# A decode step of attention with a bilinear GLU on one core: the first weight load is placed elsewhere in the ring, its projections are seven even runs, the last V heads are grouped 1-2-1, and the last gather is four steps

## The chip, the cores and the metric

The kernel runs on one core of one Trainium2 chip. The metric is the device time in microseconds (us) of one execution; a kernel's time is the median of several executions without the profiler. One further execution was profiled. The core has TensorE (PE), VectorE (DVE), ScalarE (ACT), GpSimd (POOL) and SyncE (SP); here SP issues nearly all DMA transfers, in the order in which they are written.

## The reference

One token for each of two sequences (B = 2, D = 512), all float32:

```python
xn = layernorm(x)
q = (xn @ wq)                       # 32 heads of 128
k = k_cache[:, :, 8192 - 2048:, :]  # the last 2048 positions
v = v_cache[:, :, 8192 - 2048:, :]
scores = einsum("bhqd,bhkd->bhqk", q, k) * 128 ** -0.5
o = einsum("bhqk,bhkd->bhqd", softmax(scores), v)
h = (xn @ w_gate) * (xn @ w_up)     # 1376 wide
out = x + o.reshape(B, 1, 4096) @ wo + h @ w_down
```

Every weight and every cached key and value is used once, so some 160 MB go from HBM to the core for two small output rows.

## The kernel before

**Staging.** The host lays all inputs but `x` out as one stream in the order of use. In SBUF one large tile, `step` (in the code `ring`), holds whatever is loaded: every load is one DMA of 128 rows with a run of columns for each partition. The ring has a place for four V heads (`C_V`, 16384 columns, 4096 for each head), one for four K heads (`C_K`, 16384) and 12288 columns for pairs of w_q and w_o chunks and the early rows of w_down. The table in `loads()` (L47) gives each load its semaphore, its first column and its fields. `x` is the first load (w_gate, w_up, the first chunk of w_q, and constants, 13082 columns), `k0` the four K heads of group 0, `v0` its V heads, `w1` early rows of w_down with w_q and w_o chunks, then `k1`, `v1`, `k2`, `v2`, and so on. The last ones are `v7` (V heads 28 and 29), `v30`, `v31`, and four small loads `d0`, `wo7`, `d1`, `d2`, which hold rows of w_down and the last chunk of w_o.

**Work.** Eight groups of four heads. For a group PE projects q (`q_ps`, matmuls against `xn`), multiplies q with K (`s_ps`, 32 matmuls of 512 columns), and after the softmax multiplies the weights `p` with V (`o_ps`, 32 matmuls). The profile counts two passes for each float32 matmul, so four matmuls appear as x8 and 32 as x64. `gather` takes the four blocks of `o_ps` that belong together (DVE `om`, then `red`), PE picks the rows (`pk`), DVE scales them (`oT`), and PE multiplies them with w_o (`acc`), which DVE adds to `xr`. Ahead of group 0 stand the projections for gate and up: three runs each of 459 columns. ACT copies a gate run from `q_ps` to `g`; DVE multiplies an up run with it into `h`. In group 0 PE also multiplies early rows of w_down (section `e`, `acc<-step,hT`), ahead of the V matmuls; after the last V head it multiplies further rows (section `r`) and at the end of the program the rest (section `tail`, `s_ps`).

**What sets the order.** `Program` records every operation with what it reads and writes; `plan` makes a wait of every dependence that is not known to be met. PE runs its sections in a loop whose waits (`hold`) compare a semaphore with a register. Since a wait in the loop is for one semaphore, a `relay` stands in for others: POOL waits for them and then writes a small memset into `none`, whose end raises the one that PE waits for (`wq`, `wo`, `V2`, `V3`). A load is issued by SP as soon as PE has read what lay at its place. SP works in order: a load that waits holds up all those behind it. `x` starts at `C_GU`, which is `C_V`, so that it fills the place of V, while `w1` goes to that of the pairs; `v0` is issued in the main loop after the projection of q for group 0.

Every instruction has the line of the helper that records it, L107, in the profile.

Of the kernel before, what the change touches and what calls it, by code (L numbers as in the profile page):

```python
# [5 lines left out]
ALU = mybir.AluOpType  # L6
# [19 lines left out]
CK = B * W  # L26
GW = -(-F // 3)
GU = [(w, n) for w in range(2) for n in range(3)]
CX = N + 4 + 4 + 2
# [17 lines left out]
def loads():  # L47


    v, k = [("v", h) for h in range(H)], [("k", h) for h in range(H)]  # L50
    pair = [(("wq", g), ("wo", g - 1)) for g in range(NG)]
    wd = {i: ("wd", i) for i in range(NFC + 1)}
    last = H - HG
    out = {
        "x": (None, C_GU, [("gu", t) for t in GU] + [("wq", 0), ("c", 0)]),
        "k0": ("K", C_K, k[:HG]),
        "w1": (None, C_E - len(EARLY) * D, [wd[i] for i in EARLY] + [*pair[2], *pair[1]]),
    }
    for g in range(NG - 1):
        if g:  # L60
            out[f"k{g}"] = ("K", C_K, k[g * HG : g * HG + HG])
        out[f"v{g}"] = ("V", C_V, v[g * HG : g * HG + HG])
        if g == 2:
            out["w2"] = (None, C_E, [*pair[4], *pair[3]])
        if g == 4:
            out["w4"] = (None, 0, [("wo", 6), ("wq", 7), *pair[6], *pair[5]])
# [31 lines left out]
class Op:  # L98
    def __init__(self, eng, method, args, kw, deps, dma, tag, place, holds, late):
        self.eng, self.method, self.args, self.kw, self.late = eng, method, args, kw, late  # L100
        self.deps, self.dma, self.tag, self.place, self.holds = deps, dma, tag, place, holds
# [21 lines left out]
class Program:  # L123


    def __init__(self, nc):
        self.nc = nc
        self.eng = {"PE": nc.tensor, "DVE": nc.vector, "ACT": nc.scalar,
                    "POOL": nc.gpsimd, "SP": nc.sync}
        self.ops, self.seen = [], {}  # L130
        self.tags = {}
        self.tag, self.also, self.held, self.late = None, [], [], None
        self.section, self.step = None, 0
# [23 lines left out]
    def put(self, eng, method, writes, reads, args, kw, dma=False):  # L157
# [20 lines left out]
        if tag is None:  # L178
            tag = f"d{i}" if dma else eng
        else:  # L180
            self.tags.setdefault(tag, []).append(i)
        place, holds = None, []
# [4 lines left out]
        late, self.late = self.late, None  # L187
        self.ops.append(Op(eng, method, args, kw, deps, dma, tag, place, holds, late))
        return i
# [9 lines left out]
    def plan(self, looped):  # L199
# [15 lines left out]
        for i, o in enumerate(ops):  # L215
# [20 lines left out]
            if o.dma and o.tag in self.tags:  # L236
                prev = [key_of(j) for j in self.tags[o.tag] if j < i]
                assert all(know.get(key, 0) >= val for key, val in prev), (o.tag, i)
# [7 lines left out]
        for i, o in enumerate(ops):  # L246
# [4 lines left out]
            else:  # L251
                continue
            value[o.tag] = at[i] = value.get(o.tag, 0) + step
        return waits, at

    def emit(self, looped, control):
# [10 lines left out]
        def give(i, first=None):  # L267
# [11 lines left out]
            if i in at:  # L279
                ins.then_inc(sem[o.tag], 16 if o.dma or o.tag in BY_16 else 1)  # L280

# [19 lines left out]
        once = {}  # L301
        for i in own["SP"][:3]:
            give(i)
# [7 lines left out]
        with nc.body("straight", valid_engines=list(kinds.values())):  # L311
            for e in kinds:
                here = self.eng[e].mark_branch_hint_location()
                for i in own[e][3 if e == "SP" else 0 :]:
                    if i not in stores:
                        give(i)
# [50 lines left out]
def steer(prog, regs, run):  # L367
# [8 lines left out]
    with nc.body("pe_q", valid_engines=only):  # L376
        here = pe.mark_branch_hint_location()
        regs["from"] = pe.snap(at, min_val=0, max_val=RING - 4 * FB)
        regs["by"] = pe.snap(step, min_val=GW, max_val=FB)
        run("q")  # L380
        pe.reg_add(n, n, 1)
        pe.br_lt(n, len(GU) + 2, on_true="pe_n", on_false="pe_k")
    with nc.body("pe_n", valid_engines=only):
        pe.reg_add(at, at, NC * GW)
        pe.br_lt(n, len(GU) + 1, on_true="pe_q", on_false="pe_c")
    with nc.body("pe_c", valid_engines=only):
        pe.reg_mov(step, FB)
        pe.br("pe_q")
    with nc.body("pe_k", valid_engines=only):
        pe.reg_mov(at, then)  # L390
# [24 lines left out]
def build(nc, stream, x_nat, out):  # L415
# [27 lines left out]
    hT = pr.sb("hT", [P, NFC + 1, 32])  # L443
    g_sb = pr.sb("g", [P, 3, GW])
    h_sb = pr.sb("h", [P, (NFC + 1) * P])
    o_out = red
# [25 lines left out]

    def relay(tag, *aps):
        nonlocal relays
        pr.also = list(aps)
        pool.memset(none[:, relays : relays + 1], 0.0, tag=tag)
        relays += 1
# [7 lines left out]
    issue("k0")  # L485
    issue("w1")
    for t, v in ((xr, 0.0), (eps_t, EPS), (xs, 0.0), (h_sb, 0.0), (zero, 0.0), (ones, 1.0),
                 (mt, 0.0), (qz, 0.0), (p_all, 0.0)):
        pool.memset(t, v)
    pr.load("ACT", xr[:B, :], x_nat)  # L490
    for t in (acc, q_ps, s_ps):
# [7 lines left out]
    dve.tensor_scalar(xs2, x2, total, None, ALU.subtract)  # L499
    dve.tensor_tensor(g_sb[:B, 0, 0:GW], xs2[:, 0:GW], xs2[:, 0:GW], op=ALU.mult)  # L500
    dve.tensor_tensor(
        g_sb[:B, 1, 0 : D - GW], xs2[:, GW:D], xs2[:, GW:D], op=ALU.mult
    )
    flat = g_sb.rearrange("p n i -> p (n i)")
    dve.tensor_reduce(var, flat[:B, 0:D], axis=AX.X, op=ALU.add)
    act.activation(std, var, AF.Sqrt, bias=eps_t[:B], scale=1.0 / D)
# [6 lines left out]
    def project(c0, step, *used):  # L513
        nonlocal n_run
        n_run += 1
        relay("wq", *used)
        pr.part("q")
# [8 lines left out]

    hh_ = h_sb[:B, 0 : 3 * GW].rearrange("p (n i) -> p n i", n=3)
    used = [xn]
    for i, (w, n) in enumerate(GU):
        project(C_GU + i * NC * GW, GW, got["gu", (w, n)], *used)  # L530
        wide = min(GW, F - n * GW)
        if w == 0:
            act.copy(g_sb[:B, n, 0:wide], q_ps[:B, 0:wide])
            used = [g_sb[:B, n, 0:wide]]
        else:
            dve.tensor_tensor(
                hh_[:, n, 0:wide], g_sb[:B, n, 0:wide], q_ps[:B, 0:wide], op=ALU.mult
            )
            used = [hh_[:, n, 0:wide]]
    pool.tensor_copy(cst, got["c", 0])  # L540
    pick, rmask, mask, id4 = (
# [3 lines left out]
    def queries(g):  # L545
        across(qt, q_ps.rearrange("p (h i) -> p h i", h=HG))
        at = qz[:, 0, 0:1]
# [61 lines left out]
    def gather(g):  # L609
        dve.tensor_tensor(  # L610
            om, o_ps.rearrange("p (r d) -> p r d", r=4),
            rmask.unsqueeze(2).to_broadcast([P, 4, DH]), op=ALU.mult,
        )
        dve.tensor_reduce(red, om.rearrange("p r d -> p d r"), axis=AX.X, op=ALU.add, tag="red")
        pr.part("g")
# [35 lines left out]
    for g in range(NG):  # L651
        c0 = C_Q0 if g == 0 else C_Q[(g - 1) % 2]
        project(c0, FB, ring[:, c0 : c0 + NC * FB], *used)
        queries(g)
        used = [qt]
# [20 lines left out]
        if g < NG - 1:  # L676
            for tag in ("V2", "V3"):
                relay(tag, got["v", g * HG])
            relay("wo", place)
# [4 lines left out]
        elif g == NG - 2:  # L684
            for name in ("v7", "v30", "v31"):
                issue(name)
# [22 lines left out]
def laid_out(x):  # L709
# [15 lines left out]
    wo = x["A_wo"].reshape(NG, HG, P, D)  # L725
    gu = [x[name].reshape(NC, P, F) for name in ("B_w_gate", "B_w_up")]
    wd = x["B_w_down"]

    def field(kind, i):
# [11 lines left out]
        if kind == "wd":  # L741
            return np.pad(wd[i * P : (i + 1) * P], ((0, max(0, (i + 1) * P - F)), (0, 0)))
        w, n = i
        part = gu[w][:, :, n * GW : min(n * GW + GW, F)]
        part = np.pad(part, ((0, 0), (0, 0), (0, GW - part.shape[2])))
        return part.transpose(1, 0, 2).reshape(P, NC * GW)

# [32 lines left out]
```

## Time and profile before

| what | value |
|---|---|
| median of 3 runs | 380.36 us (379.9 to 381.18) |
| the profiled execution | 382.39 us |
| its span on the core | 381.1 us |
| mean granted clock of PE | 0.821 |
| busy PE, DVE, ACT, POOL | 216.8, 61.1, 13.2, 15.7 us |
| read from HBM | 159.53 MB, 419 GB/s over the span |

Times in the profile count from the start of the span, which is 1.29 us shorter than the profiled execution. A row of the chain of waits has the start, the duration and what the chain went through; a row of the timeline adds the engine, the shapes and, in brackets, how long the engine was idle before it and what ended that. A row of the windows has a stretch of time, its length, the busy time of PE, PE's weight loads, DVE, ACT and POOL with their instruction counts (for one tile alone, of the engines that touch it), the granted clock of PE, the share of DMA and GB/s. A packet's bytes count where the packet starts, so that short windows jump between 0 and high values.

### The profile page before, as it was taken

Reading aid. Unit: us, or ns where it says so; the run is one execution under the profiler, and the core shown is the slowest. Engines: PE = TensorE matmul, PEld = TensorE weight load, DVE = VectorE, ACT = ScalarE, POOL = GpSimd, SP = SyncE. Lnnn points to the kernel's source line nnn. Section 1 sums busy time; section 2 is a strip of 40 time slices with the busy share of each in tenths; the row PEclk is TensorE's granted clock in tenths of the full one; section 3 lists DMA queues with packets and bytes.
Section 4 is the critical chain, followed back from the end, with each engine's and each line's share of the span. In section 5 each row is a group of like instructions: output and inputs, shape, how many; then the busy total and the mean of one; then the engine's idle time right before and its main releaser. Section 6 shows DMA issues by size and latency. Waiting matters only on the chain.

```text
span 381.1 us, 3091 instructions
## 1 busy us (share of the span) xinstructions
PE 216.8 (57%) x1296; PEld 52.0 (14%) x1296; DVE 61.1 (16%) x150; ACT 13.2 (3%) x26; POOL 15.7 (4%) x55
## 2 busy tenths in 40 slices
PE   0088877287718570850909771843373876186766
PEld 0011111021102120210202110200011212021211
DVE  0300142012201220120020212021020122012203
ACT  4001010000000000000000000000000000000000
POOL 3000000001000000020000000010000030000000
PEclk9999999578958996895776895668585889589998
DMA  9999959999999998999999999999999999998994
GB/s 352 462 427 398 433 207 433 440 440 440 440 440 440 440 440 385 495 440 440 427 420 392 413 440 440 433 447 440 440 440 440 441 440 433 440 440 371 411 422 187
DMA packets 3894, 159.62 MB, mean 419 GB/s; under 512 B 434, under 2 KB 562, under 8 KB 948
## 3 DMA queue, kind: packets, MB, share of 16 engines
q1 hardware_dynamic: 3888, 159.60, 97.4%
q8 instruction: 1, 0.02, 0.0%
q14 instruction: 1, 0.01, 0.0%
q10 hardware_dynamic: 4, 0.00, 0.0%
HBM read 159.53 MB, written 0.07 MB: 419 GB/s over the span
## 4 chain that ended last, share of the span: by engine, by line
DMA 71%; PE 26%; DVE 1%; issue 1%; ACT 0%; POOL 0%; POOLq 0%
DMA step<-in_stream_dram 71%; PE o_ps L107 18%; PE q_ps L107 7%; DVE h L107 0%; ACT g L107 0%; DVE red L107 0%; PE acc L107 0%; POOL none L107 0%; DVE om L107 0%; DVE xr L107 0%; PE s_ps L107 0%; PE pk L107 0%; DVE oT L107 0%; POOLq L275 0%
## 5 line engine op out<-in xcount | busy, mean ns | idle before, releaser
L107 PE MATMUL o_ps<-step,p 128*32 128x512 f32 x512 | 74.4, 743 | 55.3 <-DMA step<-in_stream_dram 55.3
L107 PE MATMUL s_ps<-step,qz 128*8 128x512 f32 x512 | 60.9, 631 | 39.6 <-DMA step<-in_stream_dram 33.2
L107 PE MATMUL q_ps<-step,xn 128*2 x112 | 56.7, 653 | 25.1 <-POOL none L107 25.1
L107 PEld LDWEIGHTS o_ps<-step,p 128*32 128x32 f32 x512 | 17.8, 133 | 106.2 <-DMA step<-in_stream_dram 59.2
L107 DVE TENSOR_TENSOR om<-o_ps,cst 128x512 f32<-128x512 f32 x8 | 5.5, 691 | 127.7 <-PE o_ps L107 127.7
L107 PEld LDWEIGHTS s_ps<-step,qz 128*8 128x8 f32 x512 | 14.1, 94 | 86.5 <-issue 76.3
L107 PEld LDWEIGHTS q_ps<-step,xn 128*2 128x2 f32 x112 | 9.8, 92 | 72.9 <-issue 72.9
L107 DVE TENSOR_REDUCE mt<-s_ps 128x1 f32<-128x512 f32 x8 | 5.5, 692 | 88.4 <-PE s_ps L107 88.4
L107 PE MATMUL acc<-step,oT 128*2 128x512 f32 x64 | 11.6, 809 | 5.6 <-POOL none L107 3.1
L107 POOL MEMSET none<- 128x1 f32 x36 | 2.6, 98 | 283.5 <-DMA step<-in_stream_dram 254.4
L107 DVE STREAM_TRANSPOSE qt<-q_ps 32x128 f32<-32x128 f32 x32 | 9.8, 307 | 26.5 <-PE q_ps L107 26.1
L107 PE MATMUL pk<-cst,red 128*128 128x8 f32 x16 | 3.2, 272 | 14.2 <-DVE red L107 14.2
L107 PE MATMUL tot<-rs,ones 128*128 128x8 f32 x16 | 3.9, 319 | 12.0 <-DVE rs L107 12.0
L107 POOL COPY step<-step 128x2048 f32<-128x2048 f32 x5 | 9.4, 1890 | 32.4 <-PE acc L107 32.4
L107 PE MATMUL top<-dg,ones 128*128 128x32 f32 x16 | 3.3, 287 | 10.3 <-DVE dg L107 10.3
L107 DVE TENSOR_TENSOR xr<-xr,acc 128x512 f32<-128x512 f32 x9 | 6.2, 688 | 17.7 <-PE acc L107 17.7
L107 ACT COPY qz<-qt 128x8 f32<-128x8 f32 x8 | 1.6, 204 | 213.2 <-DVE qt L107 213.2
L107 DVE TENSOR_REDUCE red<-om 128x128 f32<-128x512 f32 x8 | 8.2, 1019 | 0.3
L107 ACT ACTIVATE p<-t,zero 128x128 f32<-128x128 f32 x8 | 4.2, 522 | 105.2 <-DVE t L107 105.2
L107 DVE TENSOR_TENSOR h<-g,q_ps 2x459 f32<-2x459 f32 (+1 forms) x3 | 1.9, 621 | 33.5 <-PE q_ps L107 33.5
L107 DVE STREAM_TRANSPOSE sT<-s_ps 128x512 f32<-128x512 f32 x8 | 5.7, 708 | 0.0
L107 PEld LDWEIGHTS pk<-cst,red 128*128 128x128 f32 x16 | 2.5, 193 | 21.4 <-DVE red L107 21.4
(49 smaller groups left out, 44.6 us busy)
## 6 DMA issues: line engine op xcount, KB each, us to landing
step<-in_stream_dram SPq DMA_DIRECT2D x2, 4096.0 KB, 27.7
step<-in_stream_dram SPq DMA_DIRECT2D x1, 6541.0 KB, 18.6
step<-in_stream_dram SPq DMA_DIRECT2D x1, 6144.0 KB, 34.5
step<-in_stream_dram SPq DMA_DIRECT2D x1, 5376.0 KB, 49.8
step<-in_stream_dram SPq DMA_DIRECT2D x2, 2048.0 KB, 28.0
step<-in_stream_dram SPq DMA_DIRECT2D x1, 1024.0 KB, 22.3
step<-in_stream_dram SPq DMA_DIRECT2D x1, 768.0 KB, 20.2
step<-in_stream_dram SPq DMA_DIRECT2D x1, 512.0 KB, 23.1
```

Of the source, the lines that this page charges most:

```text
L107: return getattr(engine, self.method)(*args, **self.kw)
```

## The change

The places in the ring are arranged anew: V first, then 12288 columns for the pairs, then K. The first load `x` now starts at column 15551 and ends at 28645: only the first part of it, 833 columns of the first run, lies in the place of V, and the rest lies on the places of w_q, w_o and early w_down rows. gate, up and the first q chunk are put side by side (3264 columns) and cut into seven runs of 467 columns (`RUNS`, `GW`); all seven go through one ACT copy each into a tile `wide`, and the end of the copy raises `wq` itself, without a relay. DVE multiplies gate and up once, in `wide`. `v0` is issued after the first run, ahead of `w1`, and `w1` after the last run. The relays for `V2` and `V3` are replaced by two relays at the start, each of which counts for seven groups (`times`). The last V heads come as `v28`, `v29` (heads 29 and 30) and `v31`; accordingly PE waits for `V`, `V2`, `V3` ahead of heads 0, 1 and 3 of a group, where it was 0, 2 and 3. In the last group, `gather` is one multiplication by a column of the mask and three multiply-adds of 128 columns.

```diff
-GW = -(-F // 3)
-GU = [(w, n) for w in range(2) for n in range(3)]
+RUNS = 7
+WIDE = 2 * F + FB
+GW = -(-WIDE // RUNS)
...
-C_E = HG * D + NC * FB
-C_Q = (C_E + HG * D + NC * FB, C_E)
+PAIR = HG * D + NC * FB
+C_V, C_E = 0, HG * CK
+C_Q = (C_E + 2 * PAIR, C_E + PAIR)
 C_O = tuple(c + NC * FB for c in C_Q)
-C_V = C_O[0] + HG * D
-C_K = C_V + HG * CK
+C_K = C_E + 3 * PAIR
 RING = C_K + HG * CK
-C_GU = C_V
-C_Q0 = C_GU + len(GU) * NC * GW
-C_C = C_Q0 + NC * FB
+C_END = C_K - (FB - GW - CX)
+C_GU = C_END - CX - RUNS * NC * GW
...
-        "x": (None, C_GU, [("gu", t) for t in GU] + [("wq", 0), ("c", 0)]),
+        "x": (None, C_GU, [("gu", i) for i in range(RUNS)] + [("c", 0)]),
         "k0": ("K", C_K, k[:HG]),
-        "w1": (None, C_E - len(EARLY) * D, [wd[i] for i in EARLY] + [*pair[2], *pair[1]]),
+        "v0": ("V", C_V, v[:HG]),
+        "w1": (None, C_Q[1] - len(EARLY) * D, [wd[i] for i in EARLY] + [*pair[2], *pair[1]]),
...
-    out["v7"] = ("V", C_V, v[last : last + 2])
-    out["v30"] = ("V2", C_V + 2 * CK, v[last + 2 : last + 3])
+    out["v28"] = ("V", C_V, v[last : last + 1])
+    out["v29"] = ("V2", C_V + CK, v[last + 1 : last + 3])
     out["v31"] = ("V3", C_V + 3 * CK, v[last + 3 :])
...
     issue("x")
     issue("k0")
-    issue("w1")
...
+    for tag in ("V2", "V3"):
+        relay(tag, times=NG - 1)
...
-    used = [xn]
-    for i, (w, n) in enumerate(GU):
-        project(C_GU + i * NC * GW, GW, got["gu", (w, n)], *used)
-        wide = min(GW, F - n * GW)
-        if w == 0:
-            act.copy(g_sb[:B, n, 0:wide], q_ps[:B, 0:wide])
-            used = [g_sb[:B, n, 0:wide]]
-        else:
-            dve.tensor_tensor(
-                hh_[:, n, 0:wide], g_sb[:B, n, 0:wide], q_ps[:B, 0:wide], op=ALU.mult
-            )
-            used = [hh_[:, n, 0:wide]]
-    pool.tensor_copy(cst, got["c", 0])
+    for i in range(RUNS):
+        project(C_GU + i * NC * GW, GW, *([] if i else [got["gu", 0], xn]))
+        act.copy(
+            wide[:, i * GW : (i + 1) * GW], q_ps[0:32, 0:GW],
+            tag="wq" if i < RUNS - 1 else None,
+        )
+        if i == 0:
+            pool.tensor_copy(cst, got["c", 0])
+            issue("v0")
+    issue("w1")
...
-        if hh != 1:
-            pr.hold({0: "V", 2: "V2", 3: "V3"}[hh], g + 1, "landed")
+        if hh != 2:
+            pr.hold({0: "V", 1: "V2", 3: "V3"}[hh], g + 1, "landed")
...
+        else:
+            for r in range(4):
+                part, m = o_ps[:, r * DH : (r + 1) * DH], rmask[:, r : r + 1]
+                if r == 0:
+                    dve.tensor_scalar(om[:, 0, :], part, m, None, ALU.mult)
+                else:
+                    dve.scalar_tensor_tensor(
+                        red if r == 3 else om[:, r, :], part, m, om[:, r - 1, :],
+                        ALU.mult, ALU.add, tag="red" if r == 3 else None,
+                    )
...
         if g == 0:
-            issue("v0")
-            across(hT, h_sb.rearrange("p (c i) -> p c i", i=P))
+            dve.tensor_tensor(wide[:B, 0:F], wide[:B, 0:F], wide[:B, F : 2 * F], op=ALU.mult)
+            across(hT, wide[:, 0 : (NFC + 1) * P].rearrange("p (c i) -> p c i", i=P))
```

How it moves instructions is seen at three places. The first is the start of SP's queue, here before the change; a row has the operation, its tile, the partitions and columns, and the semaphores that it waits for (`s_PE` counts PE's matmuls). The loads are x, k0, w1, and then, in the row with x5, v0, k1, v1, k2, v2.

```order
L107 DMA step<-in_stream_dram 128x13082 [waits barrier_Pool_Activation_PE_DVE_SP_release]
L107 DMA step<-in_stream_dram 128x16384
L107 DMA step<-in_stream_dram 128x10752
L307 UNCONDITIONAL_BRANCH
L313 BRANCH_PREFETCH_HINT
L107 DMA step<-in_stream_dram 128x16384 [waits s_PE] x5
```

The same start of SP's queue with the change: x, k0, v0, w1, and in the row with x4 k1, v1, k2, v2.

```order
L110 DMA step<-in_stream_dram 128x13094 [waits barrier_Pool_Activation_PE_DVE_SP_release]
L110 DMA step<-in_stream_dram 128x16384
L311 UNCONDITIONAL_BRANCH
L317 BRANCH_PREFETCH_HINT
L110 DMA step<-in_stream_dram 128x16384 [waits s_PE]
L110 DMA step<-in_stream_dram 128x10752 [waits s_POOL,s_PE]
L110 DMA step<-in_stream_dram 128x16384 [waits s_PE] x4
```

v0 has moved ahead of w1, and w1 now waits for PE (the reads of the last run) and for POOL (the copy of the constants).

The second place is PE's multiplication with the four V heads of a group, before and after; a head is eight matmuls.

```order
L107 MATMUL o_ps<-step,p 32x512 [waits s_V]
L107 MATMUL o_ps<-step,p 32x512 x15
L107 MATMUL o_ps<-step,p 32x512 [waits s_V2]
L107 MATMUL o_ps<-step,p 32x512 x7
L107 MATMUL o_ps<-step,p 32x512 [waits s_V3]
L107 MATMUL o_ps<-step,p 32x512 x7
```

In the order with the change the same 32 matmuls stand so:

```order
L110 MATMUL o_ps<-step,p 32x512 [waits s_V]
L110 MATMUL o_ps<-step,p 32x512 x7
L110 MATMUL o_ps<-step,p 32x512 [waits s_V2]
L110 MATMUL o_ps<-step,p 32x512 x15
L110 MATMUL o_ps<-step,p 32x512 [waits s_V3]
L110 MATMUL o_ps<-step,p 32x512 x7
```

The wait for `V2` has moved from ahead of a group's third head to ahead of its second.

The third place is DVE's work between the last V matmul and the last w_o matmuls, before the change:

```order
L107 RECIPROCAL rec<-tot 128x8 [waits s_PE]
L107 TENSOR_TENSOR om<-o_ps,cst 128x512 [waits s_PE]
L107 TENSOR_REDUCE red<-om 128x128 [waits s_DVE]
L107 TENSOR_TENSOR oT<-pk,rec 128x8 [waits s_PE]
L107 TENSOR_TENSOR xr<-xr,q_ps 96x512
```

and with it:

```order
L110 RECIPROCAL rec<-tot 128x8 [waits s_PE]
L110 TENSOR_SCALAR om<-o_ps,cst 128x128 [waits s_PE]
L110 SCALAR_TENSOR_TENSOR om<-o_ps,cst,om 128x128 [waits s_DVE] x2
L110 SCALAR_TENSOR_TENSOR red<-o_ps,cst,om 128x128 [waits s_DVE]
L110 TENSOR_TENSOR oT<-pk,rec 128x8 [waits s_PE]
L110 TENSOR_TENSOR xr<-xr,q_ps 96x512
```

Two instructions over 512 columns have become four over 128 columns; what stands behind them is as it was.

More of the change, by code (lines that the diff above doesn't have):

```diff
@@ L98, with __init__ @@
 class Op:
-    def __init__(self, eng, method, args, kw, deps, dma, tag, place, holds, late):
+    def __init__(self, eng, method, args, kw, deps, dma, tag, place, holds, late, times):
+        self.times = times
         self.eng, self.method, self.args, self.kw, self.late = eng, method, args, kw, late
@@ L187, in put @@
         late, self.late = self.late, None
-        self.ops.append(Op(eng, method, args, kw, deps, dma, tag, place, holds, late))
+        times, self.times = self.times, 1
+        self.ops.append(Op(eng, method, args, kw, deps, dma, tag, place, holds, late, times))
         return i
@@ L252, in plan @@
                 continue
-            value[o.tag] = at[i] = value.get(o.tag, 0) + step
+            value[o.tag] = at[i] = value.get(o.tag, 0) + step * o.times
         return waits, at
@@ L301, in emit @@
         once = {}
-        for i in own["SP"][:3]:
+        for i in own["SP"][:2]:
             give(i)
@@ L313, in emit @@
                 here = self.eng[e].mark_branch_hint_location()
[L314 removed]
+                for i in own[e][2 if e == "SP" else 0 :]:
                     if i not in stores:
@@ L515, in project @@
         n_run += 1
-        relay("wq", *used)
+        if used:
+            relay("wq", *used)
         pr.part("q")
@@ L545, in queries @@
     def queries(g):
-        across(qt, q_ps.rearrange("p (h i) -> p h i", h=HG))
+        row = q_ps if g else wide[:, 2 * F : 2 * F + FB]
+        across(qt, row.rearrange("p (h i) -> p h i", h=HG))
         at = qz[:, 0, 0:1]
@@ L609, in gather @@
     def gather(g):
[L610 to L614, printed above, removed]
+        if g < NG - 1:
+            dve.tensor_tensor(
+                om, o_ps.rearrange("p (r d) -> p r d", r=4),
+                rmask.unsqueeze(2).to_broadcast([P, 4, DH]), op=ALU.mult,
+            )
+            dve.tensor_reduce(
+                red, om.rearrange("p r d -> p d r"), axis=AX.X, op=ALU.add, tag="red"
+            )
+        else:
[7 more added lines that the diff above has]
+                        ALU.mult, ALU.add, tag="red" if r == 3 else None,
+                    )
         pr.part("g")
@@ L684, in build @@
         elif g == NG - 2:
-            for name in ("v7", "v30", "v31"):
+            for name in ("v28", "v29", "v31"):
                 issue(name)
@@ L742, in field @@
             return np.pad(wd[i * P : (i + 1) * P], ((0, max(0, (i + 1) * P - F)), (0, 0)))
[L743 to L746, printed above, removed]
+        return first[:, :, i * GW : (i + 1) * GW].transpose(1, 0, 2).reshape(P, NC * GW)
     parts = [
```

59 lines of the change are left out of this document (24 added, 35 removed).

## The prediction

> **What bounds the kernel now.** I read the DMA slices of the page first, then the chain of waits, then two-microsecond windows where the slices dip.
>
> ```profile
> DMA  9999959999999998999999999999999999998994
> GB/s 352 462 427 398 433 207 433 440 440 440 440 440 440 440 440 385 495 440 440 427 420 392 413 440 440 433 447 440 440 440 440 441 440 433 440 440 371 411 422 187
> DMA 71%; PE 26%; DVE 1%; issue 1%; ACT 0%; POOL 0%; POOLq 0%
> ```
>
> The transfers run at some 440 GB/s nearly throughout, with one deep dip, the sixth slice (47.6 to 57.2 us), and the end. So the kernel is as long as its stream, plus what interrupts the stream, plus what follows its last byte. The dip in windows:
>
> ```profile
> 48.00:50.00 2.00, 1.05 (x4) 0.14 (x3) 0.62 (x1) 0.00 (x0) 0.10 (x1) 1.00 0.80 344
> 50.00:52.00 2.00, 2.00 (x6) 0.38 (x5) 0.00 (x0) 0.00 (x0) 0.00 (x0) 1.00 0.00 0
> 52.00:54.00 2.00, 1.12 (x3) 0.09 (x1) 0.82 (x3) 0.00 (x0) 0.00 (x0) 1.00 0.00 0
> ```
>
> No packet starts in four microseconds. The chain of waits says for what:
>
> ```profile
> 0.73 18.62 DMA step<-in_stream_dram
> ...
> 49.52 3.61 PE q_ps L107 x8
> ...
> 53.15 21.65 DMA step<-in_stream_dram
> ...
> 84.54 28.93 DMA step<-in_stream_dram
> ...
> 122.65 29.57 DMA step<-in_stream_dram
> ```
>
> x lands at 19.35; PE projects seven runs out of its place until 53.13; only then is v0 issued, at 53.15, and lands at 74.80. x, k0 and w1 had been through before that. After it the stream doesn't stop: v1 lands at 113.47, v2 at 152.22, 38.75 us for two loads of 8192 KB, so 19.37 us for one.
>
> **The change, part by part.**
>
> *The gap.* What it is worth is the difference of two landings. The issues of x, k0 and w1, then the third of them, and w1's time to landing:
>
> ```profile
> 0.73 1.33 SPq L107 DMA_DIRECT2D step<-in_stream_dram  x3
> 1.64 0.42 SPq L107 DMA_DIRECT2D step<-in_stream_dram  x1
> step<-in_stream_dram SPq DMA_DIRECT2D x1, 5376.0 KB, 49.8
> ```
>
> w1 lands at 1.64 + 49.8 = 51.44. This agrees with its parts: x to 19.35, k0 19.37, w1 5376/8192 of that, 12.71: 51.43. If v0 stands in the queue in time, x, k0, v0 and w1 are through at 51.44 + 19.37 = 70.81, where now they are through at 74.80. **The gap is worth 3.99 us**, for all that follows. x itself is 12 columns (6 KB) longer: 0.01 us.
>
> It goes only if each load is issued ahead of the end of the one before it. With the change the queue is full to 38.72 (k0), 58.09 (v0), 70.80 (w1), 90.2 (k1), 109.5 (v1). The issues, one by one, follow from these rows of the timeline:
>
> ```profile
> 26.16 0.53 ACT L107 COPY g<-q_ps 2x459 f32<-2x459 f32 x1 [14.27 <-PE q_ps L107]
> 26.75 0.10 POOL L107 MEMSET none<- 128x1 f32 x1 [7.18 <-ACT g L107]
> 26.98 3.60 PE L107 MATMUL q_ps<-step,xn 128*2 x8 [0.86 <-POOL none L107]
> 54.71 7.05 PE L107 MATMUL s_ps<-step,qz 128*8 128x512 f32 x64 [1.59 <-ACT qz L107]
> 65.27 2.51 PE L107 MATMUL acc<-step,hT 128*2 128x512 f32 x10
> 74.84 9.63 PE L107 MATMUL o_ps<-step,p 128*32 128x512 f32 x64 [7.06 <-DMA step<-in_stream_dram]
> 94.70 7.05 PE L107 MATMUL s_ps<-step,qz 128*8 128x512 f32 x64 [1.60 <-ACT qz L107]
> ```
>
> v0 waits for the first run alone, over at 26.1: 12.6 us ahead of 38.72. Each of the six further runs costs PE 3.60, ACT 0.53 (467 columns for 459, no more than 0.01) and, without the relay, some 0.15 of semaphore, about 4.3; the last ends at 26.1 + 25.8 = 51.9. w1 is issued then, 6.1 ahead of 58.09; its wait for POOL is older. The last run's copy (0.53), transposes and the copy into qz (1.58 from 53.13 to 54.71) put K's matmuls at 54.1 to 61.2; k1 follows, 9.6 ahead of 70.80. Queued behind w1's wait on SP are k1 and v1, and neither is due before it. The new tail of this is section `e`: it needs w1, now behind v0, so it starts at 70.85 and no longer at 65.27, and V's matmuls behind it on PE wait too: 70.85 + 2.51 + 9.63 = 83.0, where v1 is issued, 7.2 ahead of 90.2. Scores of group 1 began 10.2 after V's matmuls ended (84.47 to 94.70): 93.2 to 100.3, and k2 follows, 9 ahead of 109.5. From there each group is paced by its landing as now. So every other edit of this stage costs nothing, hidden behind these 6 to 12 us: the relays gone, `h` (three products of 0.62) in one product of 1376, at most 1.9 us of DVE between 54 and 61. If one cover failed, the price is what it is late by, up to 3.99.
>
> *The tail.* v31 lands at 370.60, and the page's end is chain. Its rows:
>
> ```profile
> 370.64 3.41 PE o_ps L107 x16
> ...
> 374.08 0.70 DVE om L107
> ...
> 374.80 1.03 DVE red L107
> ...
> 376.61 1.08 PE acc L107 x8
> ...
> 378.46 0.66 PE s_ps L107 x16
> ```
>
> The sixteen passes of the last head took 3.41, since the clock had fallen. The head before it, and its window beside that of the last:
>
> ```profile
> 365.75 1.92 PE L107 MATMUL o_ps<-step,p 128*32 128x512 f32 x16 [0.34 <-DMA step<-in_stream_dram]
> 370.64 3.36 PE L107 MATMUL o_ps<-step,p 128*32 128x512 f32 x16 [2.96 <-DMA step<-in_stream_dram]
> 364.00:366.00 2.00, 1.66 (x20) 0.36 (x16) 0.00 (x0) 0.00 (x0) 0.00 (x0) 1.00 1.06 451
> 370.00:372.00 2.00, 1.36 (x8) 0.40 (x12) 0.00 (x0) 0.00 (x0) 0.00 (x0) 0.54 1.02 420
> ```
>
> After 2.96 idle the granted clock was 0.54; without that the same work takes 1.92. With the change heads 29 and 30 both wait for one load, which ends where v30 now lands (365.75, since the bytes ahead are the same), so they run 365.75 to 369.4 and PE idles 1.2 instead of 2.96. The clock should then hold: 3.41 − 1.92 = 1.49 less. The row that bounds this from the other side is a gather, where PE idles 1.87, does 0.39 of work and idles again:
>
> ```profile
> 86.35 0.39 PE L107 MATMUL pk<-cst,red 128*128 128x8 f32 x2 [1.87 <-DVE red L107]
> 84.00:92.00 8.00, 1.89 (x8) 0.14 (x8) 0.69 (x1) 0.00 (x0) 0.79 1.02 442
> 122.00:130.00 8.00, 1.04 (x8) 0.14 (x8) 0.69 (x1) 0.00 (x0) 1.00 1.15 500
> ```
>
> These two windows, of `acc` alone, show the same eight passes slow after such a pause in group 0 (1.89) and quick in group 1 (1.04). So a pause of two microseconds may cool PE. Head 28 alone leaves such a pause (363.6 to 365.75); a clock lost there would be back by 370, since PE works 3.6 us in between. I take the warm value, nearer to 1.2 idle; the bound is 0.
>
> [...]
>
> The gather was 1.75 (374.08 to 375.83). The trace has no multiply-add; the nearest rows:
>
> ```profile
> L107 DVE TENSOR_TENSOR t<-sT,nm 128x128 f32<-128x128 f32 x8 | 2.3, 292 | 0.3
> L107 DVE TENSOR_TENSOR om<-o_ps,cst 128x512 f32<-128x512 f32 x8 | 5.5, 691 | 127.7 <-PE o_ps L107 127.7
> L107 DVE TENSOR_TENSOR oT<-pk,rec 128x8 f32<-128x8 f32 x8 | 1.3, 166 | 3.9 <-PE pk L107 3.9
> ```
>
> Four of 0.166 to 0.691, with three gaps of 0.04, are 0.78 to 2.88; I take the 128x128 form, 4 × 0.292 + 0.12 = 1.29, so 0.46 less (0.97 less to 1.13 more).
>
> [...]
>
> Together 1.49 + 0.46 = 1.95. But what is late next are the small loads behind v31:
>
> ```profile
> 352.67 0.43 SPq L107 DMA_DIRECT2D step<-in_stream_dram  x1
> 353.62 0.43 SPq L107 DMA_DIRECT2D step<-in_stream_dram  x1
> step<-in_stream_dram SPq DMA_DIRECT2D x1, 1024.0 KB, 22.3
> step<-in_stream_dram SPq DMA_DIRECT2D x1, 256.0 KB, 23.2
> ```
>
> wo7 lands at 374.97 and d2 at 376.82. `acc` began at 376.61, 1.64 after wo7; the block with d2's rows at 378.46, 1.64 after d2. With 0.04 to react, **the tail gains 1.60**, not 1.95. A quicker gather gains no more, and one 0.35 slower than taken costs nothing.
>
> *The sum.* 3.99 + 1.60 = 5.59, call it 5.6: the profiled execution goes from 382.39 (span 381.1 and 1.29 around it) to 376.8. The median of the runs, 380.36, is 2.03 below the profiled one; the gap is the same order of work in both, so I take 5.6 from it too: **374.8 us**, 1.5% less.
>
> **The rivals.**
>
> *A cold tail.* PE is slow again at v31, or was quick in the unprofiled runs already. For it: group 0's row. Against: 1.2 us of pause, after 3.6 of work. Then the tail gains 0.46, and the time is 380.36 − 4.45 = 375.9.
>
> *The change doesn't open the gap.* If v0 in effect waited for the last run (its place and the runs overlap by more than I read), it would be issued at 51.9 instead of 53.15 and the gap would shrink by 1.2 alone: 380.36 − 1.2 − 1.6 = 377.6. For it: one shared count of PE's matmuls serves all of SP's waits. Against: only 833 of the first run's columns lie in V's place.
>
> *Slower: the first load.* Its rows now start at column 15551 and not at a multiple of 512; if writing such rows took longer, everything waits, since all PE work begins with x. x takes 18.62 for eight rows on each of sixteen queues, some 2 us a row. The change turns into a loss once a row takes 0.7 us longer (8 × 0.7 = 5.6); at double the time of a row it costs 16, 390.8. For it: no row of the trace shows such a place. Against: x's rows in HBM already start off every round boundary (52328 bytes each), and x still moves 6541 KB in about the time that k0's rate gives (15.5 us, and some 2.5 to start).
>
> **How the numbers follow.** Forecast 374.8: 0.58. Cold tail 375.9: 0.27. Gap not opened 377.6: 0.08. Slow first load: 0.07, of which 0.03 lies near no change and 0.04 beyond it. A measurement of this kernel can tell about 0.3% (1.1 us) from no change. So faster 0.93, same 0.03, slower 0.04. The range holds the first two cases. Below 374.8 I allow 1.8: half the runs' spread (0.65), and 1.1 if the unprofiled tail is not that of the profile. Above, from 375.9, the same spread and up to 0.75 for a gather at its slow bound (1.13 more in place of 0.46 less, beside a cold PE): 373.0 to 377.3.
>
> **What would show it.** In the profile with the change: no dip in the sixth DMA slice; v0 issued near 23 to 26 and w1 near 52; V's matmuls of group 0 starting near 73.4, behind `e`, and of group 1 near 109.5 and no longer 113.5; the last head's passes in 1.9, the gather in 1.3, and `acc` waiting for wo7 and no longer for `oT`. I am wrong if x lands later than 19.5, if a slice after the first group falls below 390 that didn't before, or if V of group 1 starts after 111.

## The result and the profile after

The changed kernel takes **376.59 us** (median of 4 executions, 376.03 to 377.11) where before took 380.44 in the same comparison: a ratio of 0.9897, 95% interval 0.9875 to 0.9919, so 3.9 us less (3.1 to 4.8). The forecast was 374.8 in a range of 373.0 to 377.3. The profiled execution went from 382.39 to 377.11 and its span from 381.1 to 375.7, close to the 376.8 and 375.5 of the sum. That the profile agrees so well and the median is 1.8 us above the forecast is the puzzle of this study.

The page's slices of DMA after the change:

```profile
DMA  9999999999999999999999999999999999999995
GB/s 357 462 447 398 426 416 435 481 440 419 405 426 433 447 447 401 485 447 398 419 426 440 447 447 419 419 461 412 426 433 447 447 447 440 447 398 396 441 408 215
```

The dip is gone: the sixth slice moves 416 GB/s where it moved 207. The issue of v0, from the timeline, and the chain of waits through the first stage and the end:

```profile
23.21 0.34 SPq L110 DMA_DIRECT2D step<-in_stream_dram  x1
0.74 18.53 DMA step<-in_stream_dram
...
25.69 3.61 PE q_ps L110 x8
29.30 0.02 issue
29.32 0.55 ACT wide L110
29.87 0.13 issue
30.00 3.61 PE q_ps L110 x8
...
50.83 19.86 DMA step<-in_stream_dram
...
81.38 28.01 DMA step<-in_stream_dram
...
346.64 8.79 PE s_ps L110 x64
...
359.17 9.74 PE o_ps L110 x64
368.91 0.03 issue
368.94 0.36 DVE om L110
...
370.09 0.36 DVE red L110
...
371.24 1.08 PE acc L110 x8
```

v0 is issued at 23.21, a run takes 4.31 (25.69 to 30.00), w1 is issued at 50.83 and lands at 70.69, v1 lands at 109.39: the first stage is as worked out, to within 0.2 us of 70.80 and 109.5. (v0 could go before the first run had ended, at 25.00, since only the run's first part lies in V's place.) The end is not as worked out. The scores of group 7 took 8.79 us, and its 64 V passes 9.74 without a pause: PE was still on them, until 368.91, when v31 had landed at 366.02. No wait for v31 or wo7 is in the chain.

### The profile page after: what moved, and what is told of

The parts are those of the page before. It is cut to its first block, busy times and chain, and to the rows that moved or that the text cites. A ratio compares the mean times of both kernels' runs of the same rounds, so it can differ in the third digit from the quotient of the medians.

```text
span 375.7 us, 3064 instructions
## 1 busy us (share of the span) xinstructions
PE 216.8 (58%) x1296; PEld 52.4 (14%) x1296; DVE 60.4 (16%) x149; ACT 15.4 (4%) x30; POOL 13.4 (4%) x37
## 4 chain that ended last, share of the span: by engine, by line
DMA 65%; PE 30%; DVE 2%; ACT 1%; issue 1%; POOL 0%; POOLq 0%
DMA step<-in_stream_dram 65%; PE s_ps L110 13%; PE q_ps L110 8%; PE o_ps L110 7%; PE acc L110 2%; ACT wide L110 1%; DVE om L110 0%; DVE red L110 0%; DVE qt L110 0%; PE pk L110 0%; DVE mt L110 0%; DVE xr L110 0%; DVE sT L110 0%; PE tot L110 0%; ACT p L110 0%
## 5 line engine op out<-in xcount | busy, mean ns | idle before, releaser
L110 PE MATMUL o_ps<-step,p 128*32 128x512 f32 x512 | 73.6, 730 | 46.0 <-DMA step<-in_stream_dram 46.0
L110 PE MATMUL s_ps<-step,qz 128*8 128x512 f32 x512 | 62.8, 647 | 38.8 <-DMA step<-in_stream_dram 33.5
L110 DVE STREAM_TRANSPOSE qt<-q_ps 32x128 f32<-32x128 f32 x28 | 8.6, 306 | 24.1 <-PE q_ps L110 23.8
L110 POOL MEMSET none<- 128x1 f32 x18 | 1.5, 99 | 229.1 <-DMA step<-in_stream_dram 216.1
L110 DVE STREAM_TRANSPOSE qt<-wide 32x128 f32<-32x128 f32 x4 | 1.2, 302 | 37.2 <-ACT wide L110 37.2
L110 DVE TENSOR_REDUCE red<-om 128x128 f32<-128x512 f32 x7 | 7.1, 1018 | 0.2
L110 PE MATMUL acc<-step,hT 128*2 128x512 f32 (+1 forms) x10 | 3.6, 1040 | 5.2 <-DMA step<-in_stream_dram 5.2
```

The costliest lines, as they stand in the source:

```text
L110: return getattr(engine, self.method)(*args, **self.kw)
```

## The experiments

Three theories were set against each other. Theory 1 is the prediction: the gap is worth 4.0 and the tail 1.6 in every execution. Theory 2: the gap gives nearly all, and the tail next to nothing, because what PE's clock does there differs from one execution to the next, and the first profile of before caught a costly one. Theory 3: the tail gives its 1.6 and the gap only 2.3.

### The kernel before, profiled again

No edit.

> The kernel before, unchanged, profiled once more. The median gain (3.85 us) is smaller than the profiled one (5.28 us). If the tail of the first profile was typical, its last V head again takes about 3.4 us and the span is again near 381 us. If that execution was a slow one (theory: the clock at the last V head varies from one execution to the next), the span is nearer to 379 us and the last head takes 1.7 to 2.5 us.

Its span was 379.1 us. The timeline of PE around the last two groups of matmuls:

```profile
349.84 8.75 PE L107 MATMUL s_ps<-step,qz 128*8 128x512 f32 x64 [3.78 <-DMA step<-in_stream_dram]
359.86 0.41 PE L107 MATMUL top<-dg,ones 128*128 128x32 f32 x2 [1.28 <-DVE dg L107]
361.77 0.59 PE L107 MATMUL tot<-rs,ones 128*128 128x8 f32 x2 [1.50 <-DVE rs L107]
362.29 9.71 PE L107 MATMUL o_ps<-step,p 128*32 128x512 f32 x64
```

This is the same kernel as in the prediction, whose scores took 7.05 and whose last head then waited 2.96 us. Here PE's clock was low in the scores (granted 0.65 between 350 and 352, 0.50 between 352 and 354), PE came to V 0.5 us later and slow again, and all 64 passes ran through; there is no pause ahead of v31 and nothing for the new grouping to mend. The last head took no 3.4 us, as theory 2 has it.

### The two edits of the end alone, and all but them

The kernel before with the new grouping and the new gather:

```diff
-    out["v7"] = ("V", C_V, v[last : last + 2])
-    out["v30"] = ("V2", C_V + 2 * CK, v[last + 2 : last + 3])
+    out["v28"] = ("V", C_V, v[last : last + 1])
+    out["v29"] = ("V2", C_V + CK, v[last + 1 : last + 3])
...
-        if hh != 1:
-            pr.hold({0: "V", 2: "V2", 3: "V3"}[hh], g + 1, "landed")
+        if hh != 2:
+            pr.hold({0: "V", 1: "V2", 3: "V3"}[hh], g + 1, "landed")
...
+            for r in range(4):
+                part, m = o_ps[:, r * DH : (r + 1) * DH], rmask[:, r : r + 1]
...
```

> The kernel before with the two edits of the end alone: heads 28, 29-30, 31 and the gather in four steps. Theory 1 (as predicted: gap 4.0, tail 1.6 in every execution): 1.6 us below before, ratio 0.9958. Theory 2 (the gap gives all, the tail next to nothing in the median, because PE's clock there is not always cold before and not always warm after): 0 to 0.5 us below, ratio 0.9987 to 1.000. Theory 3 (the tail gives 1.6 and the gap only some 2.3): 1.6 us below.

The changed kernel with both edits undone (the same lines the other way round), and with the grouping alone undone:

> The changed kernel with V heads 28-29, 30, 31 and the gather in two steps, as before: the new placing and order of the loads alone. Theory 1: 4.0 us below before, ratio 0.9895, and 1.6 us above the changed kernel. Theory 2: 3.6 to 4.0 us below before, equal to the changed kernel within 0.4 us. Theory 3: 2.3 us below before, ratio 0.994.

> The changed kernel with V heads 28-29, 30, 31 as before, but the gather in four steps. Theory 1 (the grouping keeps the clock up at the last head): 1.1 to 1.5 us above the changed kernel, that is 2.3 to 2.8 us below before. Theory 2: equal to the changed kernel within 0.4 us, 3.4 to 4.0 us below before.

| kernel | median (executions) | ratio to before, 95% interval |
|---|---|---|
| before, new end | 380.88 (12) | 0.9994 (0.9973 to 1.0015) |
| changed, old end | 376.22 (6) | 0.9886 (0.9855 to 0.9917) |
| changed, old grouping | 376.46 (6) | 0.9895 (0.9863 to 0.9926) |

Before stood at 380.91 beside them (17 executions, 379.32 to 382.32). The end alone gives 0.2 us, between 1.0 less and 0.6 more; everything but the end gives 4.3, as much as the whole change (3.9 above, 4.3 in the second comparison below). Theories 1 and 3 fall: both need 1.6 from the end. How the last head ran with the old end, in the chain of the changed kernel with the old end:

```profile
365.76 1.97 PE o_ps L110 x16
...
367.75 0.70 DVE om L110
...
368.48 1.03 DVE red L110
```

The old end's last head took 1.97 here, not 3.41.

### How late may v0 be?

The first load placed lower by 3 or 5 runs, so that v0 waits for run 3 or run 5 (here for 3 runs; for 5 it is `5 * NC * GW` and `i == 5`):

```diff
-C_END = C_K - (FB - GW - CX)
+C_END = C_K - (FB - GW - CX) - 3 * NC * GW
...
-                 (qz, 0.0), (ring[:, C_END:C_K], 0.0), (p_all, 0.0)):
+                 (qz, 0.0), (ring[:, C_END : C_END + FB - GW - CX], 0.0), (p_all, 0.0)):
...
             pool.tensor_copy(cst, got["c", 0])
+        if i == 3:
             issue("v0")
```

> The changed kernel with the first load placed three runs lower, so that runs 0 to 2 and the first part of run 3 lie in V's place and v0 waits for run 3. By the queue (theory: only a break in the stream costs): v0 is issued near 36, before k0 has landed at 38.7, so nothing or at most 0.3 us is lost: 376.5. Rival (an earlier v0 helps in itself, by whatever path): 10 us or more of the 13 us that v0 is later are lost or a fair part of them, above 378.

> The same with five runs: v0 waits for run 5 and is issued near 44.7, 6 us after k0 has landed. By the queue: v0 lands 21.65 us after its issue, near 66.3 where it would be 58.0, so 8.3 us are lost, on the whole stream: 384.8, and the last landing moves by as much. Rival (part of a break is made good later, since PE has slack): clearly less than 8.

The issue of v0, first with 3 runs, then with 5:

```profile
36.23 0.34 SPq L110 DMA_DIRECT2D step<-in_stream_dram  x1
```

```profile
44.21 0.34 SPq L110 DMA_DIRECT2D step<-in_stream_dram  x1
```

With 3 runs the kernel took 377.07 (4 executions, 376.20 to 377.31; ratio 0.9892, 0.9852 to 0.9933). That is 0.5 to 0.9 above the changed kernel's two medians (376.59 and, below, 376.20) and above the 0.3 expected; two of the four executions, 377.27 and 377.31, are slower than all ten of the changed kernel. The profile shows a loss of 0.6: the last load landed 353.6 us after x, where it is 353.0 in both profiles of the changed kernel. Some 0.3 of it is there when v0 lands, at 58.06: it was issued 2.1 us ahead of k0's landing (38.37), and that was a little late. Still, 13 us of delay cost next to nothing. With 5 runs v0 was issued 5.8 us after k0 had landed (38.41), and the kernel took 384.89 (4 executions; ratio 1.0109, 1.0069 to 1.0150): 8.3 to 8.7 more, 8.3 expected. The last load landed 361.3 us after x, 8.3 later than in the changed kernel. So a late v0 cost next to nothing (0.6) when it was issued 2.1 us ahead of the end of what was queued. Issued behind that end it cost all of its lateness: the 5.8 us, and the 2.5 that this load into an empty queue took longer (21.84 where the stream took 19.37). Nothing of this break was made good later in the stream.

### Keeping PE's clock up ahead of the scores

Sixteen idle matmuls ahead of each group's scores, into a bank that nothing reads:

```diff
+WARM = 16
...
         pr.part("k")
+        for _ in range(WARM):
+            pe.matmul(warm[:, 0:P], ones, ones, start=True, stop=True)
         pr.hold("K", g + 1, "landed")
```

> The changed kernel with sixteen idle matmuls of 128 columns into an unused bank ahead of the scores of each group, which keep PE's clock up while it waits for K. Theory 2 (the scores of the last group run cold after their pause, PE then reaches the last V head late, and that is why the tail gains nothing): scores of group 7 take 7.1 and no longer 8.8 us, PE waits for the last heads, and the time falls by 0.4 to 1.0 us below the changed kernel. Rival (the small loads behind v31 bound the end in any case): the same time within 0.3 us. If the sixteen matmuls themselves get in the way: 0.5 to 1.5 us slower.

> The same sixteen matmuls with V heads 28-29, 30, 31 and the gather in two steps, as before the change. Theory 2: with warm scores PE pauses some 3 us ahead of the last head, whose matmuls then take 3.4 us, so this is 1.0 to 1.6 us slower than with the new tail. Rival (the two edits of the end are worth nothing in any state of the clock): equal to it within 0.4 us.

Both were slower than the changed kernel, 378.47 (10 executions) and 378.50 (11). The scores of group 7 took 7.05 in both, as meant, and the last head, from the timelines of the first and of the second kernel:

```profile
365.63 1.92 PE L111 MATMUL o_ps<-step,p 128*32 128x512 f32 x16 [1.25 <-DMA step<-in_stream_dram]
370.01 1.04 PE L111 MATMUL acc<-step,oT 128*2 128x512 f32 x8 [0.43 <-DMA step<-in_stream_dram]
373.83 0.29 PE L111 MATMUL s_ps<-step,hT 128*2 128x128 f32 x1 [1.93 <-issue]
```

```profile
365.96 1.92 PE L111 MATMUL o_ps<-step,p 128*32 128x512 f32 x16 [1.72 <-DMA step<-in_stream_dram]
374.32 0.27 PE L111 MATMUL s_ps<-step,hT 128*2 128x128 f32 x1 [2.10 <-issue]
```

Two readings. The last head took 1.92 with either end, after pauses of 1.25 and 1.72. That is no test of the grouping at a high clock throughout: the V passes ran slow again in both profiles (in the first the first 16 took 3.60, where 16 quick ones take 1.92; in the second the first 48 took 7.05, where three times 1.92 are 5.76), so that PE came to the last head with less to wait than the 2.96 of the first profile of before. With the new end `acc` did wait for wo7 (0.43), as predicted, so what the gather saved was partly lost there. And PE stood still for some 2 us amid its last matmuls, waiting for nothing that the profile shows, which hid any gain. So I tried it with four matmuls of 512 columns:

```diff
+WARM = 4
...
+        for _ in range(WARM):
+            pe.matmul(warm, ones, zero.to_broadcast([P, FB]), start=True, stop=True)
```

> The changed kernel with four idle matmuls of 512 columns ahead of each group's scores, in place of sixteen short ones, since with those the program's last matmuls stood still for 1.9 us with nothing waited for, which hid what the clock gave. Theory 2: scores of group 7 take 7.1 us, PE waits for the last heads and for wo7, the span less the last landing is 2.6 us, 0.5 to 0.8 us less than the changed kernel in its cold form; median 375.8 to 376.2. If the standing still comes back: 378.

> The same four idle matmuls with heads 28-29, 30, 31 and the gather in two steps. With warm scores: if PE's clock drops in the pause ahead of the last head as in the first profile of before (2.96 us), the last head takes 3.4 us and this is 1.0 to 1.6 us slower than with the new tail. If the pause is shorter (1.7 us, as with sixteen idle matmuls), the last head takes 1.9 us, only the gather (0.2 us) and the wait for wo7 differ, and the two are equal within 0.4 us.

376.53 and 376.17 (6 each; ratios 0.9888 with intervals 0.9864 to 0.9913 and 0.9864 to 0.9912). The standstill was gone, and the two ends did not differ here either; the old one's last head waited 1.84 and took 1.92, after 48 V passes in 7.03. The first is not faster than the changed kernel: in its profile the idle matmuls themselves came late (345.63 to 349.34) and held up the scores. No kernel of this study beats the changed one clearly.

### The changed kernel again

> The changed kernel, unchanged, more executions and a second profile. All theories: 376.0 to 377.1, the median near 376.4, its last landing near 372.1. If the tail of the first profile is typical (scores of group 7 cold, 8.8 us), the span less the last landing is again 3.4 us; if the other one (PE not paused ahead of the scores), 2.6 us.

376.20 (6 executions, 375.96 to 376.83; ratio 0.9888, 0.9864 to 0.9912), span 374.7. This time the scores ran at a high clock, PE came early, and the new grouping showed what it does. PE in the timeline, and the windows with the granted clock (the third figure from the right):

```profile
346.32 7.05 PE L110 MATMUL s_ps<-step,qz 128*8 128x512 f32 x64 [3.22 <-DMA step<-in_stream_dram]
356.88 1.92 PE L110 MATMUL o_ps<-step,p 128*32 128x512 f32 x16
360.85 7.05 PE L110 MATMUL o_ps<-step,p 128*32 128x512 f32 x48 [2.05 <-DMA step<-in_stream_dram]
360.00:362.00 2.00, 1.15 (x12) 0.42 (x16) 0.00 (x0) 0.00 (x0) 0.00 (x0) 0.96 1.00 426
362.00:364.00 2.00, 2.00 (x12) 0.43 (x8) 0.00 (x0) 0.00 (x0) 0.00 (x0) 0.50 0.98 418
364.00:366.00 2.00, 2.00 (x16) 0.56 (x12) 0.00 (x0) 0.00 (x0) 0.00 (x0) 0.69 0.95 397
```

Head 28 alone makes a pause of 2.05 us ahead of heads 29 and 30. The clock fell to 0.50 after it, and the 48 passes took 7.05 us, to 367.9: the grouping moved the pause from the last head to the second one. In the changed kernel with the old end, PE was through at 367.7. That 0.2 and the 0.2 that the new gather saves cancel: `acc` began at 370.27 here and at 370.29 with the old end. (The kernel with v0 behind run 5 had the same pause, 2.04, and the same 7.05.)

### Is it PE's clock that set the stream of before?

The kernel before with fourteen idle matmuls while PE waits for x:

```diff
+    pr.part("w")
+    for _ in range(14):
+        pe.matmul(warm, ones, zero.to_broadcast([P, FB]), start=True, stop=True)
...
+    run("w")
     pe.br("pe_q")
```

> The kernel before with fourteen idle matmuls on PE while it waits for x, and nothing else changed. Theory (before, the end of the stream is v0's issue plus some 323.8 us, and v0's issue hangs on how long PE's clock is low in the first projection): the first run takes 3.6 us and no longer 5.4 to 6.4, v0 is issued near 50.2 to 50.6, the last landing is at 374.0 to 374.4, and the time falls by 1.5 to 2.5 us to some 378.5, with a smaller spread than before. Rival (the spread of before comes from the transfers themselves): v0's issue moves but the last landing doesn't follow it, or the spread stays at 3 us.

The rows that answer it: the first run, v0's issue, the issue of d2 and d2's time to landing, and the place of the standstill.

```profile
19.38 3.59 PE L107 MATMUL q_ps<-step,xn 128*2 x8 [0.99 <-POOL none L107]
49.99 0.33 SPq L107 DMA_DIRECT2D step<-in_stream_dram  x1
350.61 0.43 SPq L107 DMA_DIRECT2D step<-in_stream_dram  x1
step<-in_stream_dram SPq DMA_DIRECT2D x1, 256.0 KB, 23.2
377.55 0.57 PE L107 MATMUL s_ps<-xr,cst 128*2 128x128 f32 x8 [2.35 <-issue]
```

v0 was issued at 49.99 and d2 landed at 350.61 + 23.2 = 373.81. Set beside the other profiles of the old loading order, each last landing worked out in that way:

| profile | first run | v0 issued | last landing | difference | span less last landing |
|---|---|---|---|---|---|
| before | 6.42 | 53.15 | 376.82 | 323.67 | 4.28 |
| before, again | 5.39 | 51.67 | 375.50 | 323.83 | 3.60 |
| before, new end | 5.80 | 52.20 | 376.16 | 323.96 | 3.44 |
| before, warm start | 3.59 | 49.99 | 373.81 | 323.82 | 6.69 |

The end of the stream follows v0's issue to within 0.3 us. v0's issue follows the first run: in all four it is x's landing (19.35, 18.92, 19.02, 19.02) plus the first run plus 27.4 us. And the first run follows PE's clock: its first passes took 1.06 us each and the later ones 0.59, as in every run after it, with six slow ones of eight in the first profile of before, four in the second and none after the warm start. (A window from 19 to 26 says 1.00 in the first profile of before, but the trace has no record of the clock ahead of 25.43.) The time itself did not fall: 381.86 (12 executions, 379.62 to 383.54; ratio 1.0031, 1.0008 to 1.0053), against the 378.5 expected, and the spread stayed. In the profile (span 380.5) the standstill of 2.35 ate most of the 3.0 us by which the stream ended earlier than in the first profile of before, and the last head, after a pause of 2.98, took 3.48 (3.36 there). So the mechanism of the stream is shown, and that a warm start helps is not; nor is it shown that the first run's clock makes the spread of before.

With the new loading order (changed, changed again, with the old end, with the old grouping, and the two with four idle matmuls) the last landing was at 371.93 to 372.30 in six profiles, while w1 was issued between 50.2 and 51.5: it no longer depends on PE. Counted from x's landing it was 353.0 us in all six. Behind it the span went on for 3.4 us in the first profile of the changed kernel (375.7 − 372.30), 2.8 in the second, 2.7 with the old end and 2.6 with the old grouping: the first of the four had slow scores in group 7 (8.75), the others quick ones (7.05).

## Why the prediction was right, and which term was mis-sized

- **The gap** was right in mechanism and size. Predicted 3.99; the last landing moved by 4.52 between the two first profiles and from a mean of 376.16 (three profiles of the old order, the warm start left out) to 372.05 (six): 4.1. Counted from x's landing it is 4.0 (357.1 to 353.0). The dose (0.6 for 13 us of delay, 8.3 for 21) confirms that only the break counted. One condition was too mild: issued 2.1 us ahead of the end of the load before it, v0 still landed some 0.3 late. All leads of the change are longer (7.1 at the least, for w1).
- **The covers** held: w1, `e` (70.73), V of group 0 behind it and k1, v1 came in time, as did the edits costed at nothing.
- **The tail** was mis-sized. The step "the tail gains 1.60, not 1.95" had 1.49 from the clock at the last head and 0.46 from the gather. Measured: 0.2, between a loss of 0.6 and a gain of 1.0. Its first part took a single execution for the rule. For the state of that execution it was nearly right: 4.28 us behind the last landing there, 2.8 in the changed kernel's second profile, where the scores were quick too. But among the seven profiles with the old grouping the last head was slow in the first one of before and with the warm start, and not in before again, the changed kernel with the old end or grouping, or the two variants of the old end with idle matmuls ahead of the scores. Where the scores or the V passes ran at a low clock, PE came late and had a short pause (1.84 at most) or none; where PE came early in the changed kernel, the new grouping made its own pause of 2.05 us and the clock fell to 0.50 there. The sentence that "a clock lost there would be back by 370" saw it, but not that some 0.2 us of the lost time stay. (The 1.49 is also 0.05 too much: it sets 3.41 from the chain against 1.92 from the timeline, where the same passes have 3.36.)
- **The gather** took 1.51 and not 1.29 (368.94 to 370.45): a multiply-add of 128 columns takes 0.36 us, where the 128x128 row that I took has 0.29. It saves 0.24.
- **wo7 as the next bound** was seen with the old grouping (0.44 of waiting) and with sixteen idle matmuls (0.43), both with the new gather, where PE was early; in both profiles of the changed kernel `acc` waited for `oT`.
- **The transfer to the median** is where the tail's mistake shows. 5.6 us were worked out from one execution and taken off the median of others. The gap lost nothing by that (4.0 predicted, 4.1 measured); the tail fell from 1.6 to 0.2. The profiled execution of before had both a late v0 (53.15, where others had 51.67 and 52.20) and a slow last head; its 382.39 lie at the top of the 379.3 to 382.6 that before shows. What the change took from it, 5.28, is more than what it takes from the median. That this is so close to 5.6 was luck: of the 5.4 us that the profiled span lost, 4.5 lie ahead of the last landing and 0.9 behind it, where 4.0 and 1.6 were worked out.
- **The rivals.** The case held likeliest, 374.8, is not the one that came. The cold tail's time, 375.9, was the nearest. Of its two wordings the second, that PE "was quick in the unprofiled runs already", is the nearer to what the runs show: in the second profile of before no pause slowed the last head, and the end alone gave 0.2. The first load did not become slower (x landed at 0.74 + 18.53 = 19.27, with 19.35 before), and v0 did not wait for the last run. (In the arithmetic of that rival the start of x is 3.1, 18.62 less 15.5, and not 2.5.)

What PE's pauses showed: the one of 2.05 us had the drop to 0.50 behind it, and so had the gather's 1.87 in group 0's row in the prediction (the clock was 0.50 from 86.87 on), while behind the 1.72 us of the second warm variant and the 1.84 of the last the head was quick (1.92). The traces of before and of the changed kernel show more of it. Their records of the granted clock hold 1.00 and 0.50 alone, and each of the 60 changes in them comes 3.41 us or a whole multiple of it (up to 12) behind the one before or behind the start of the record. The record starts at 25.43 in the one and at 23.22 in the other, so that the places of the changes, counted back by 3.41, lie 1.53 and 2.74 us behind the start of the span. PE in such stretches of 3.41 us, in the second profile of the changed kernel and in that with four idle matmuls and the old end (PE's busy time, then the granted clock):

```profile
358.43:361.84 3.41, 1.36 (x16) 1.00 0.98 418
361.84:365.26 3.42, 3.42 (x24) 0.50 0.96 406
```

```profile
363.64:367.06 3.42, 1.58 (x20) 1.00 0.96 400
367.06:370.47 3.41, 2.19 (x20) 1.00 0.97 397
```

The first window holds the pause of 2.05 and PE was busy for 0.40 of it; the clock was 0.50 in the next. The third holds the 1.84, with 0.46 busy, and the clock stayed. In the traces of before and of the changed kernel, cut at the changes into stretches of 3.41 us, PE was busy for at most 0.54 of the stretch ahead of a fall (30 falls) and for at least 0.45 of one behind which a high clock stayed (97 stretches); for at least 0.84 of the one ahead of a rise (30) and for at most 0.75 of one behind which a low clock stayed (48). (The first two overlap between 0.45 and 0.54; some matmul records can be missing from a trace.) So the length of a pause alone didn't tell a fall here, and the busy share of a stretch told it better; what causes a fall is not shown. In the first profile of before the stretch ahead of the last head (366.76 to 370.17) had PE busy for 0.27.

Two things stay open: why the stream from the end of the first stage to d2 is up to 0.5 us shorter with the new order (372.30 − 70.69 = 301.61, and 301.5 to 301.7 in six profiles, where before had 376.82 − 74.80 = 302.02, and 301.7 to 302.1 in four), and why the kernels with 14 or 16 more matmuls in PE's program stood still. For the second no row shows a cause: the pages of these three have one packet of 0.02 MB on the queue `q8 instruction`, but so have those of before (it starts at 377.79 there) and of the changed kernel (372.33), without a standstill.

## What to carry to other kernels

When a kernel is as long as its stream, look for the one break in it and count for each load how long before the end of the queue it is issued: here a lead of 2.1 us cost 0.6 beside one of some 15, and a lack of 5.8 us cost its full length and 2.5 us more. Loads that waited for a compute engine also inherited that engine's clock: v0 was issued at 53.15 behind a first run of 6.42, and at 49.99 behind one of 3.59. The kernel whose queue runs ahead was steadier as well as faster (1.1 us of spread over 10 executions, 3.2 over many more of before), but that the first run's clock made the spread is not shown, since it stayed with the warm start. An end that depends on a matmul clock is not to be sized from one execution: profile before twice, and take a term off the median only if both show it.

## What the runs showed of the hardware

- A load of 8192 KB into an empty queue landed 2.3 to 2.7 us later than one that stood behind another (21.65 to 22.11 for v0 in the four profiles of the old order, 21.84 with 5 runs, where a load in the stream took 19.37).
- In the traces of before and of the changed kernel the granted clock was 1.00 or 0.50, and its 60 changes lay 3.41 us or whole multiples of it apart. Ahead of a fall PE was busy for at most 0.54 of 3.41 us (30 falls), ahead of a rise for at least 0.84 (30 rises). A pause of 2.05 us ahead of a V head had a fall behind it, pauses of 1.72 and 1.84 had none.
- With 14 or 16 matmuls more in its program, PE stood still for 1.93 to 2.35 us amid its last section; with 4 more it didn't. What causes it was not tried.
